# A polynomial-sketch attention fused with a SiLU feed-forward: one planned order for all engines, block-transposed layouts, one SiLU per two banks

## The chip, the cores and the metric

The kernel runs on one core of one Trainium2 chip. The metric is device time in microseconds (us) of one execution. "Profile" is a page and a trace of one execution, taken by the hardware profiler. Engines in it: PE is TensorE's matmuls, PEld its weight loads, DVE is VectorE, ACT is ScalarE, POOL is GpSimd, SP is SyncE (here it only issues DMAs). L352 is line 352 of the kernel profiled.

## The reference, cut to what matters

```python
batch, n_heads, seq, head_dim = 4, 4, 1088, 32      # r = 8
# attention without softmax: phi(x) = outer(S1 x, S2 x), 64 features per head
q_p, k_p = phi(q), phi(k)
kv  = einsum('bhsf,bhsd->bhfd', k_p, v);  z = k_p.sum(axis=2)
num = einsum('bhsf,bhfd->bhsd', q_p, kv)
den = einsum('bhsf,bhf->bhs',  q_p, z)[..., None] + 1e-06
x   = (num / den).transpose(0, 2, 1, 3).reshape(4352, 128)
# feed-forward
h = x @ w_in              # 128 -> 2048
g = h * sigmoid(h)        # SiLU
out = g @ w_out           # 2048 -> 128
```

The feed-forward has 2048 hidden columns, 16 tiles of 128 partitions, for 4352 tokens: 68 blocks of 128 x 1024. "Block" means such a block of `h` from here on; both kernels hold it in one PSUM tile of 2 x 512 fp32 columns (`h_ps`; `psA` or `psB`), and a half of such a tile is called a bank here.

## The kernel before

Attention runs batch by batch in tiles of 128 tokens, in fp32, with bf16 outer products shared by VectorE and GpSimd. The leftover 64 tokens of each batch (1088 = 8 x 128 + 64) are tiles of their own. Then comes the feed-forward, in chunks of 512 tokens; a scheduler may move its work up between the attention's. Its inner loop:

```python
for jp in range(NJ // 2):
    h_ps = psA.tile([P, 2, CH], FP32, name="h_ps", tag="h")          # two of these
    for jj in range(2):
        nc.tensor.matmul(h_ps[:, jj, :ntok], w_in_bf[:, j * P: (j + 1) * P], xT[:, t0: t0 + ntok], ...)
    s_sb = moe.tile([P, 2, CH], BF16, name="s_sb", tag="s")
    nc.scalar.activation(out=s_sb[:, :, :ntok], in_=h_ps[:, :, :ntok], func=ACT.Sigmoid)
    g_j = moeg.tile([P, 2, CH], BF16, name="g_sb", tag="g")
    nc.vector.tensor_tensor(out=g_j[:, :, :ntok], in0=h_ps[:, :, :ntok], in1=s_sb[:, :, :ntok], op=ALU.mult)
# ... 16 matmuls into outT_ps, a VectorE block transpose, 4 stores
```

and the projection of the queries, 128 tokens at a time, in fp32:

```python
nc.tensor.matmul(pq_ps[:nt, i, :], QT[:, t * P: t * P + nt], WQb, start=True, stop=True)   # 96 columns
```

## Time and profile before

Two runs: 198.16 and 195.95 us, median 197.06.

| what | value | where it is read |
|---|---|---|
| busiest engine | VectorE, 68% of the span | page, busy time |
| first sigmoid | 46.3 us | source view of its line |
| sigmoid, 128 x 1024 | 1.02 us | groups by line |
| multiply, 128 x 1024 | 1.21 us | groups by shape |
| DMA packets under 512 B | 71,424 of 72,075 | page, slices |

From the page of the kernel before: the span, each engine's busy time, and some rows of the span cut into 40 equal slices (4.9 us each). A digit is the busy share in tenths; PEclk is the granted TensorE clock in tenths of full speed.

```profile
span 196.7 us, 2161 instructions
...
PE 130.4 (66%) x674; PEld 73.1 (37%) x684; DVE 134.3 (68%) x239; ACT 95.5 (49%) x134; POOL 45.3 (23%) x100
...
PE   1085479744875999865767744859885757657660
...
DVE  4335644783678372998779897675478787787961
ACT  2001011347665233777755668363566757576560
PEclk9999999999998555999999999576999999999998
...
DMA packets 72075, 11.15 MB, mean 57 GB/s; under 512 B 71424, under 2 KB 71424, under 8 KB 71936
```

No engine is near full, so waiting sets the time. ScalarE does little in the first nine slices: the feed-forward has not begun. From slice 14 on the clock is at half for some slices, and again later.

From the page, the chain that ended last (by line) and the two costliest groups. Columns of a group: line, engine, operation, output<-input, shape, count | busy us, mean ns | idle us before it and what ended the idle time.

```profile
DVE g_sb L357 17%; ACT s_sb L355 12%; SPq L155 10%; SPq L147 10%; PE h_ps L352 8%; PE outT_ps L362 6%; SPq L164 5%; PE pq_ps L251 4%; PE pk_ps L184 3%; DVE o_tt L366 2%; DMA Qxx<-in_q_dram 2%; PE num_ps L305 1%; PE zacc L195 1%; DVE qp_b L290 1%; PE qpt_ps L299 1%
...
L357 DVE TENSOR_TENSOR g_sb<-h_ps,s_sb 128x1024 bf16<-128x1024 f32 (+1 forms) x72 | 81.3, 1154 | 19.8 <-ACT s_sb L355 18.9
L355 ACT ACTIVATE s_sb<-h_ps 128x1024 bf16<-128x1024 f32 (+1 forms) x72 | 70.1, 977 | 36.0 <-PE h_ps L352 31.0
```

The multiply is 81.3 of VectorE's 134.3 us. VectorE waits for the sigmoid (18.9 us in all), the sigmoid waits for `h` (31.0 us), and the matmul for `h` waits for the multiply (22.6 us by the page), which is the last to read the bank pair: a ring.

From the timeline of the kernel before, two pairs of 512-column matmuls (start us, duration us):

```profile
50.33 1.06 PE L352 MATMUL h_ps<-xT,w_in_bf 128*128 128x512 bf16 x2
...
143.74 0.59 PE L352 MATMUL h_ps<-xT,w_in_bf 128*128 128x512 bf16 x2
```

The same pair took 1.06 us and 0.59 us. A duration here is longer than the step from one matmul to the next: a single such matmul takes 0.38 us in the second state and 0.63 in the first (in the changed kernel's warm-up). So the step is about 1.06 - 0.63 = 0.43 us in the first case and 0.59 - 0.38 = 0.21 in the second. The first pair ran at half clock, although PEclk shows 9 at 50 us: the trace holds no clock record before about 52 us, and the row shows full speed until the first record. For the first part of a trace the matmuls' own spacing has to be read.

### The profile page before, as it was taken

What the parts mean: (1) busy time and instruction counts of PE and PEld (TensorE: products, weight loads), DVE (VectorE), ACT (ScalarE), POOL (GpSimd) and SP (SyncE); (2) the same over time, 40 slices, a digit from 0 to 9 for tenths busy, and PEclk for the clock granted to TensorE, in tenths of its full rate; (3) what the DMA queues carried; (4) which work ended last, traced back from release to release, by engine and by line L of the source; (5) the groups of instructions that cost most, each with busy time, mean ns of one, the idle gap of its engine ahead of it and who ended that gap; (6) DMA issues with size and microseconds to landing.
All of it is one profiled execution on the core that took longest, in us unless ns stands there. A gap on an engine that the chain in (4) does not pass through costs nothing.

```text
span 196.7 us, 2161 instructions
## 1 busy us (share of the span) xinstructions
PE 130.4 (66%) x674; PEld 73.1 (37%) x684; DVE 134.3 (68%) x239; ACT 95.5 (49%) x134; POOL 45.3 (23%) x100
## 2 busy tenths in 40 slices
PE   1085479744875999865767744859885757657660
PEld 1074468521322765422226522723331212212330
DVE  4335644783678372998779897675478787787961
ACT  2001011347665233777755668363566757576560
POOL 1173263871000431540007360170000000000000
PEclk9999999999998555999999999576999999999998
DMA  2989799779994000003000000003213012030031
GB/s 40 146 133 146 117 217 309 128 118 154 131 139 68 7 0 0 2 4 50 3 0 0 2 0 3 0 0 53 35 19 53 0 21 36 0 55 0 0 53 27
DMA packets 72075, 11.15 MB, mean 57 GB/s; under 512 B 71424, under 2 KB 71424, under 8 KB 71936
## 3 DMA queue, kind: packets, MB, share of 16 engines
q1 hardware_dynamic: 72064, 11.02, 38.1%
q8 instruction: 5, 0.08, 0.2%
q14 instruction: 6, 0.05, 0.1%
HBM read 8.79 MB, written 2.23 MB: 56 GB/s over the span
## 4 chain that ended last, share of the span: by engine, by line
SPq 26%; PE 25%; DVE 22%; ACT 15%; issue 5%; DMA 2%; POOL 2%; DVEq 0%; ACTq 0%; POOLq 0%
DVE g_sb L357 17%; ACT s_sb L355 12%; SPq L155 10%; SPq L147 10%; PE h_ps L352 8%; PE outT_ps L362 6%; SPq L164 5%; PE pq_ps L251 4%; PE pk_ps L184 3%; DVE o_tt L366 2%; DMA Qxx<-in_q_dram 2%; PE num_ps L305 1%; PE zacc L195 1%; DVE qp_b L290 1%; PE qpt_ps L299 1%
## 5 line engine op out<-in xcount | busy, mean ns | idle before, releaser
L357 DVE TENSOR_TENSOR g_sb<-h_ps,s_sb 128x1024 bf16<-128x1024 f32 (+1 forms) x72 | 81.3, 1154 | 19.8 <-ACT s_sb L355 18.9
L355 ACT ACTIVATE s_sb<-h_ps 128x1024 bf16<-128x1024 f32 (+1 forms) x72 | 70.1, 977 | 36.0 <-PE h_ps L352 31.0
L352 PE MATMUL h_ps<-xT,w_in_bf 128*128 128x512 bf16 (+1 forms) x138 | 42.9, 393 | 24.2 <-DVE g_sb L357 22.6
L362 PE MATMUL outT_ps<-g_sb,w_out_bf 128*128 128x512 bf16 (+1 forms) x140 | 43.7, 395 | 8.6 <-DVE g_sb L357 6.9
L352 PEld LDWEIGHTS <-w_in_bf 128*128 128x128 bf16 x144 | 14.2, 104 | 43.1 <-issue 26.4
L362 PEld LDWEIGHTS <-w_out_bf 128*128 128x128 bf16 x144 | 14.4, 103 | 25.9 <-issue 15.6
L201 POOL TENSOR_TENSOR kp_b<-pk_sb 128x256 bf16<-128x256 f32 x16 | 12.5, 802 | 43.8 <-ACT pk_sb L188 43.8
L184 PE MATMUL pk_ps<-WK,KT 128*128 128x64 f32 (+1 forms) x72 | 15.6, 381 | 8.4 <-DVE KT L175 8.4
L201 DVE TENSOR_TENSOR kp_b<-pk_sb 128x256 bf16<-128x256 f32 (+1 forms) x20 | 11.6, 614 | 11.0 <-ACT pk_sb L188 10.6
L251 PE MATMUL pq_ps<-WQb,QT 128*128 128x96 f32 (+1 forms) x72 | 16.8, 394 | 1.2 <-ACT pq_sb L258 1.2
L184 PEld LDWEIGHTS pk_ps<-WK,KT 128*128 128x128 f32 (+1 forms) x72 | 13.9, 283 | 10.0 <-DVE KT L175 9.5
L188 ACT ACTIVATE pk_sb<-pk_ps 128x256 f32<-128x256 f32 x8 | 3.1, 383 | 29.0 <-PE pk_ps L184 28.9
L220 POOL CAST vbf<-vraw 128x128 bf16<-128x128 f32 (+1 forms) x36 | 12.5, 366 | 14.9 <-DMA vraw<-in_v_dram 14.4
L251 PEld LDWEIGHTS pq_ps<-WQb,QT 128*128 128x128 f32 (+1 forms) x72 | 13.7, 281 | 4.0 <-ACT pq_sb L258 3.4
L290 DVE TENSOR_TENSOR qp_b<-aqs,pq_sb 128x256 bf16<-128x256 f32 (+1 forms) x20 | 10.8, 574 | 1.2 <-POOL aqs L282 0.6
L290 POOL TENSOR_TENSOR qp_b<-aqs,pq_sb 128x256 bf16<-128x256 f32 x16 | 11.3, 727 | 0.6
L258 ACT ACTIVATE pq_sb<-pq_ps 128x384 f32<-128x384 f32 x8 | 3.9, 490 | 14.6 <-PE pq_ps L251 11.7
L299 PE MATMUL qpt_ps<-ident_bf,qp_b 128*128 128x128 bf16 (+1 forms) x72 | 7.7, 244 | 5.0 <-ACT xT L308 4.7
L366 DVE STREAM_TRANSPOSE o_tt<-outT_ps 128x512 f32<-128x512 f32 (+1 forms) x9 | 6.1, 681 | 6.4 <-PE outT_ps L362 5.6
L299 PEld LDWEIGHTS <-qp_b 128*128 128x128 bf16 (+1 forms) x72 | 5.3, 108 | 9.9 <-issue 6.7
L308 ACT ACTIVATE xT<-num_ps 128x512 bf16<-128x512 f32 (+1 forms) x12 | 5.7, 475 | 6.1 <-PE num_ps L305 6.1
L195 PE MATMUL zacc<-pk_sb 128*32 128x32 f32 (+1 forms) x72 | 5.9, 233 | 4.0 <-ACT pk_sb L188 2.8
(69 smaller groups left out, 87.6 us busy)
## 6 DMA issues: line engine op xcount, KB each, us to landing
Kxx<-in_k_dram SPq DMA_DIRECT2D x16, 136.0 KB, 3.9
Qxx<-in_q_dram SPq DMA_DIRECT2D x16, 136.0 KB, 4.1
vraw<-in_v_dram SPq DMA_DIRECT2D x32, 64.0 KB, 3.2
out_dram<-o_tt SPq DMA_DIRECT2D x32, 64.0 KB, 2.0
w_in_f<-in_moe_w_in_dram SPq DMA_DIRECT2D x1, 1024.0 KB
vraw<-in_v_dram SPq DMA_DIRECT2D x4, 32.0 KB, 2.3
out_dram<-o_tt SPq DMA_DIRECT2D x4, 32.0 KB, 1.7
L_111<-in_S_dram SPq DMA_DIRECT2D x4, 1.0 KB
```

The source lines that it names most:

```text
L147: nc.sync.dma_start(Kxx[D * h: D * (h + 1), :, :], sap)
L155: nc.sync.dma_start(vt[:nt], v[b, :, t * P: t * P + nt, :].rearrange("h s d -> s h d"))
L184: nc.tensor.matmul(pk_ps[:nt, i, :], KT[:, t * P: t * P + nt], WK, start=True, stop=True)
L201: beng.tensor_tensor(out=kp[:nt], in0=_insert_bcast(ak4, 2, R), in1=_insert_bcast(bk4, 1, R), op=ALU.mult)
L220: nc.gpsimd.tensor_copy(out=vb[:nt], in_=Vraw[t][:nt])
L251: nc.tensor.matmul(pq_ps[:nt, i, :], QT[:, t * P: t * P + nt], WQb, start=True, stop=True)
L290: beng.tensor_tensor(out=qp[:nt], in0=_insert_bcast(aqs[:nt, i], 2, R), in1=_insert_bcast(bq4, 1, R), op=ALU.mult)
L299: nc.tensor.transpose(qpt_ps[:, p, c0: c0 + nt], in_, ident_bf[:nt, :nt])
L352: nc.tensor.matmul(h_ps[:, jj, :ntok], w_in_bf[:, j * P: (j + 1) * P], xT[:, t0: t0 + ntok], start=True, stop=True)
L355: nc.scalar.activation(out=s_sb[:, :, :ntok], in_=h_ps[:, :, :ntok], func=ACT.Sigmoid)
L357: nc.vector.tensor_tensor(out=g_j[:, :, :ntok], in0=h_ps[:, :, :ntok], in1=s_sb[:, :, :ntok], op=ALU.mult)
L362: nc.tensor.matmul(outT_ps[:, :ntok], w_out_bf[:, j, :], g_sb[j // 2][:, j % 2, :ntok], start=(j == 0), stop=(j == NJ - 1))
```

## The change

The intent: take the multiply and its PSUM read out of the ring, batch the attention's small operations, make every feed-forward block full, and fix one order of instructions for all engines.

The diff rewrites nearly the whole kernel; this is its core, with cuts marked `# ...`.

```diff
+class Plan:                       # a list scheduler: every op has an engine, an assumed cost and a due time
+    def order(self):
+        # ... for each op whose inputs are planned: earliest start t from engine, inputs, free banks
+                if best is None or (t < best[0] - 1e-9) or (t <= best[0] + 1e-9 and (o.due, o.idx) < best[3]):
+                    best = (t, o, got, (o.due, o.idx))
+        # ... the ops sorted by planned start are then emitted in that order on all engines
-            nc.scalar.activation(out=s_sb[:, :, :ntok], in_=h_ps[:, :, :ntok], func=ACT.Sigmoid)
-            nc.vector.tensor_tensor(out=g_j[:, :, :ntok], in0=h_ps[:, :, :ntok], in1=s_sb[:, :, :ntok], op=ALU.mult)
+                A_.activation(out=gt[int(s[0][1:])], in_=hp, func=ACTF.Silu)
+            a = op(f"S_{i}_{s_}", "ACT", 0.92, fa, [l1], due + 0.93 * s_ + 0.5, need=[("g", 1)], frees=[l1])
+            l2 = op(f"L2_{i}_{s_}", "PE", 0.435, f2, [a, wo[...], seq.get("l2")], due + 0.93 * s_ + 1.5, ...)
+    for i in range(9):             # warm-up matmuls on zeros
+        wk.append(op(f"warm{i}", "PE", 0.43, lambda s: mm(bank(7), warm[:, 0:128], warm), [warmz], -20 + i * 0.01))
+    def proj8(name, W, src, deps, due):          # batches 1 to 3: 8 tiles of 64 rows x 32 columns of the array
+        # ...
+                    mm(bank(s[P])[32 * j:32 * j + 32, 0:256].rearrange("p (g x) -> p g x", g=2),
+                       W[64 * P:64 * P + 64].rearrange("p x h i -> p (x h i)"),
+                       src[64 * P:64 * P + 64, :, j].rearrange("p g c t -> p g (c t)"),
+                       tile_position=(64 * P, 32 * j))
+            dt = op(f"QD{b}{hf}", "SP", 0.5, lambda s, i=i, hf=hf: nc.sync.dma_start_transpose(
+                out=QPT[i][:, 4 * hf:4 * hf + 4].rearrange("p c q t -> p (c q) t"),
+                in_=qp[i][:, 4 * hf:4 * hf + 4].rearrange("p c h f -> p (c h f)")), ...)
+    chunk("r", col, 256, xr, None, t0)           # the 4 x 64 leftover tokens as one last chunk
```

Four consecutive tokens lie beside each other on a partition now, so a load moves runs of 256 or 512 bytes. The weights and V are cast to bf16 by the DMA (from the POOL queue). VectorE transposes between token and feature layout, which the program lays out in blocks of 32. Batch 0 takes another way, with TensorE transposes and full-array projections, 128 tokens at a time; it has to be first and quick. "Head" is the time until the first SiLU.

## The prediction

> **What bounds the kernel now.** The page gives no engine above 68% of the 196.7 us span (VectorE 134.3 us, TensorE 130.4, ScalarE 95.5); waiting sets the time.
>
> (1) Head: by the source view, the first sigmoid starts at 46.3 us. Attention of batches 0 and 1 goes first, behind 128-byte DMA packets (71,424 of 72,075 under 512 B; the 40-slice row shows the DMA busy until about 60 us) that one queue issues.
>
> (2) Then 64 full and 8 half blocks. Between 140 and 186 us the timeline shows 1.3 to 1.45 us per 1024 columns: matmul, sigmoid (1.02 us), VectorE multiply out of the same PSUM pair (1.21 us), only then is the bank free. By group, the multiply costs 81.3 us and is 17% of the chain of waits; "h_ps waits for g_sb" is 20.9 us. Between 62 and 80 us only 4 sigmoids ran: fp32 attention matmuls (8 take 1.5 to 2 us) came first, at a granted clock of 0.53.
>
> **Removed.** The multiply and one PSUM read per block: SiLU is one ScalarE pass. POOL's products go (45.3 us POOL; VectorE's 128x256 products took 0.64 us beside POOL, 0.41 at least). Weight casts move into the DMA. 68 full blocks, no half ones. Input packets of 256 to 512 B.
> **Added.** 6 DMA transposes (no duration in this trace), head transposes on TensorE, block transposes on VectorE (128x512: 0.68 us), warm-up matmuls.
>
> **Costs after.** ScalarE: consecutive 128x1024 activations start about 0.92 us apart in the chain view: 68 x 0.92 = 63 us. [...] So SiLU should cost what sigmoid did. TensorE: four 512-column matmuls 0.213 us apart (timeline, full clock): 0.86 us a block, 58 us in all. Estimated extra per batch from trace pieces: KV products 18 x 83 ns = 1.5, z 0.7, projections 2, numerators 0.9, about 5.5 us; three batches, plus later parts of batch 0 and leftovers (7): 58 + 17 + 7 = 82 us. VectorE: about 14 us per batch of 18 to 19, not the limit. TensorE becomes the limit, ScalarE second.
>
> **Sum.** First SiLU at about 16 us (K by 5, then some fifteen short dependent operations); stream 84 us with few waits; tail 4 us (matmuls, copy, store about 2). Total **104 us**, 8-in-10 range **94 to 118**. Chances: faster by over 2% 0.98, within 2% 0.01, slower 0.01.
>
> **What would show it.** First SiLU at 13 to 20 us; 68 SiLUs of 1.0 to 1.03 us, mean start to start 1.15 to 1.3 us; TensorE over 80% busy in the stream, clock near 1 (it fell to 0.5 before after slices with little matmul work); VectorE 60 to 70%, POOL almost nothing; ScalarE waits for h (TensorE), not VectorE; the chain mostly matmuls of the two layers.
>
> **What would make it wrong.** DMA transposes landing after 4 us or more: [...] The order follows assumed costs; one underestimated item blocks an engine while others have work. The 64x32 tiles may not overlap (projections 3 us, not 1: +10 us). Casting loads from POOL could be slow: head over 20 us. Half clock after a stall (0.9 us more per block). On the good side, less TensorE work than I add up: 92 us.

The sum came to 16 + 84 + 4 = 104 us. The 63 us for ScalarE come from the 0.92 us of the trace. No trace of the kernel before has a SiLU, so that it should cost what sigmoid did was my assumption. The 4 us, the 3 us for projections and the 20 us for casting loads are fears, not measurements; what came of them is told under "Why the prediction was wrong". The fall of the clock to 0.5 is in the trace: TensorE was busy for 0.70 of the 2 us from 60 to 62 us, and from about 62 to 79 us the clock was at half.

## The result, and the profile after

Two runs: 121.17 and 121.28 us; median 121.22. The ratio to the kernel before is 0.6152 (95% interval 0.6003 to 0.63). All ratios here are the mean time of one kernel's fast runs over that of the other's fast runs of the same rounds, so not quite the ratio of the medians. Faster was right, by a wide margin; 121.2 us lies outside the range of 94 to 118.

From the page of the changed kernel, the same parts as before, with slices of 3.0 us:

```profile
span 119.4 us, 2011 instructions
...
PE 106.1 (89%) x745; PEld 59.6 (50%) x753; DVE 60.0 (50%) x149; ACT 71.6 (60%) x80; POOL 17.3 (14%) x33
...
PE   5978999997997899999999999989998998898930
...
ACT  0442210100568965609877777888979989889840
PEclk9995555555599999999999999999999999999998
...
DMA packets 43177, 10.58 MB, mean 89 GB/s; under 512 B 34688, under 2 KB 43168, under 8 KB 43168
...
PE ps L256 28%; DMA KL<-in_k_dram 20%; ACT gt L496 17%; PE psA L256 9%; PE psB L256 7%; DMA Qr<-in_q_dram 4%; DMA QPT<-qp 3%; DMA K<-in_k_dram 3%; DVE KT L683 1%; SPq L261 1%; DVE AQ L717 1%; DVE kp L367 1%; DVE Mq L729 0%; ACT orest L527 0%; ACTq L496 0%
```

TensorE is now the full engine, as predicted. But the PEclk row has eight slices at half clock, about 9 to 33 us, and ScalarE's row starts in earnest only at the eleventh slice. (The chain's DMA share lies before 33 us, where it is followed back along the loading queue. TensorE was busy all along, and the first experiment moves the head without touching a load.)

The source view of the SiLU line. Columns: operation, count, duration ns min/median/max, first and last start us, shapes:

```profile
L496 ACT ACTIVATE gt<-psB x34: 1017/1021/1030, 31.3 to 112.2; 128x1024 bf16<-128x1024 f32 x34
L496 ACT ACTIVATE gt<-psA x34: 1017/1024/1030, 32.2 to 113.5; 128x1024 bf16<-128x1024 f32 x34
```

So 68 SiLUs of 1.02 us as predicted, but the first starts at 31.3 us, not 16. The last ends at 113.5 + 1.02 = 114.5: the stream took 83.2 us, against 84 predicted. The tail took 119.4 - 114.5 = 4.9 us, against 4. Against the prediction: head +15.3, stream -0.8, tail +0.9, and 1.8 us between the span and the device time, in all 17.2. The miss is the head.

Three windows in the head. Columns: window, its length, busy us (instructions) of PE, PEld, DVE, ACT and POOL, granted clock, DMA share, GB/s:

```profile
10.00:15.00 5.00, 4.54 (x33) 3.89 (x33) 3.30 (x7) 1.45 (x4) 2.84 (x5) 0.50 1.36 207
15.00:20.00 5.00, 5.00 (x24) 4.82 (x24) 2.51 (x6) 0.37 (x1) 3.30 (x5) 0.50 1.43 226
20.00:25.00 5.00, 5.00 (x51) 3.80 (x51) 3.47 (x10) 0.59 (x1) 2.12 (x3) 0.50 1.55 210
```

TensorE is busy for nearly the whole of each window, at half clock. I had taken it that a busy TensorE keeps its full clock; this one did not. The timeline of the same stretch shows with what it is busy (start us, duration us):

```profile
14.35 1.97 PE L256 MATMUL psA<-Wh,Q0T 128*128 128x64 f32 x8
...
16.81 1.97 PE L256 MATMUL ps<-Wh,Q0T 128*128 128x64 f32 x8
18.57 1.86 PE L256 MATMUL psA<-MQ,Q0T 128*128 128x32 f32 x8
...
25.31 0.63 PE L256 MATMUL ps<-V,kp 128*128 128x64 bf16 x8
```

These are mostly fp32 matmuls of 64 and 32 columns, each behind an fp32 weight load (the eight of the first line took 1.78 us): the PEld column above is 4.82 of 5 us from 15 to 20 us. The KV matmuls of batch 0, which the first chunk needs, come only at 25.3 us, behind the projections of later queries. The trace shows no wait for V there: the two loads of batch 0's V had landed by 12.8 us (issued at 4.6 and 5.4, landed 7.3 to 7.5 us later). It was the planned order that put them late.

Late in the stream, where no attention is left, the timeline of the changed kernel shows this order:

```profile
96.81 1.02 ACT L496 ACTIVATE gt<-psB 128x1024 bf16<-128x1024 f32 x1
96.96 0.59 PE L256 MATMUL ps<-gt,w_out 128*128 128x512 bf16 x2 [0.26 <-ACT gt L496]
...
97.39 0.59 PE L256 MATMUL psA<-xT,w_in 128*128 128x512 bf16 x2
...
98.08 1.02 ACT L496 ACTIVATE gt<-psA 128x1024 bf16<-128x1024 f32 x1 [0.26 <-PE psA L256]
...
99.00 1.02 ACT L496 ACTIVATE gt<-psB 128x1024 bf16<-128x1024 f32 x1
```

After the SiLU of psA ends (96.91), TensorE first does the second-layer matmuls of that block and only then refills psA; ScalarE idles 0.26 us in each pair. A pair of blocks takes 99.00 - 96.81 = 2.19 us, 1.10 per block, though SiLUs on end start 0.92 us apart (98.08 and 99.00).

### The profile page after: what moved, and what is told of

It is laid out like the page before. It is cut to its first block, busy times and chain, and to the rows that moved or that the text cites. A ratio compares the mean times of both kernels' runs of the same rounds, so it can differ in the third digit from the quotient of the medians.

```text
span 119.4 us, 2011 instructions
## 1 busy us (share of the span) xinstructions
PE 106.1 (89%) x745; PEld 59.6 (50%) x753; DVE 60.0 (50%) x149; ACT 71.6 (60%) x80; POOL 17.3 (14%) x33
## 2 busy tenths in 40 slices
DMA packets 43177, 10.58 MB, mean 89 GB/s; under 512 B 34688, under 2 KB 43168, under 8 KB 43168
## 4 chain that ended last, share of the span: by engine, by line
PE 44%; DMA 29%; ACT 17%; DVE 3%; issue 2%; SPq 1%; ACTq 0%; another core or an unknown queue 0%
PE ps L256 28%; DMA KL<-in_k_dram 20%; ACT gt L496 17%; PE psA L256 9%; PE psB L256 7%; DMA Qr<-in_q_dram 4%; DMA QPT<-qp 3%; DMA K<-in_k_dram 3%; DVE KT L683 1%; SPq L261 1%; DVE AQ L717 1%; DVE kp L367 1%; DVE Mq L729 0%; ACT orest L527 0%; ACTq L496 0%
## 5 line engine op out<-in xcount | busy, mean ns | idle before, releaser
L496 ACT ACTIVATE gt<-psB 128x1024 bf16<-128x1024 f32 x34 | 34.7, 1021 | 18.2 <-PE psB L256 17.7
L496 ACT ACTIVATE gt<-psA 128x1024 bf16<-128x1024 f32 x34 | 34.8, 1022 | 8.6 <-PE psA L256 6.1
L256 PE MATMUL ps<-gt,w_out 128*128 128x512 bf16 (+1 forms) x141 | 36.3, 355 | 3.2 <-ACT gt L496 2.8
L256 PEld LDWEIGHTS <-w_in 128*128 128x128 bf16 x160 | 15.5, 100 | 16.1 <-issue 3.3
L256 PEld LDWEIGHTS <-w_out 128*128 128x128 bf16 x144 | 12.8, 97 | 18.2 <-issue 10.6
L256 PE MATMUL psB<-xT,w_in 128*128 128x512 bf16 (+1 forms) x81 | 20.6, 351 | 0.6 <-ACT gt L496 0.4
L256 PE MATMUL psA<-xT,w_in 128*128 128x512 bf16 (+1 forms) x74 | 19.8, 358 | 0.2
L367 DVE TENSOR_TENSOR kp<-AB 128x512 bf16<-128x512 f32 x16 | 10.4, 680 | 3.4 <-ACT AB L450 3.4
L367 DVE TENSOR_TENSOR qp<-aqs,AQ 128x512 bf16<-128x512 f32 (+1 forms) x14 | 9.5, 719 | 0.1
L261 POOL DMA_DIRECT2D V<-in_v_dram x8 | 6.1, 759 | 2.7 <-DMA w_out<-in_moe_w_out_dram 2.7
```

The costliest lines, as they stand in the source:

```text
L256: P_.matmul(out_, lhsT, rhs, start=start, stop=stop, **kw)
L261: return op(name, eng, 1.0 if eng == "POOL" else 0.5, lambda s: e.dma_start(dst, src), deps, due, xfer=kb * 1.024 / rate)
L367: V_.tensor_tensor(out=dst, in0=bcast(a, 2, R), in1=bcast(b_, 1, R), op=ALU.mult)
L496: A_.activation(out=gt[int(s[0][1:])], in_=hp, func=ACTF.Silu)
```

## The experiments

Every run gave correct results. The kernels in one group ran on the same chip with their own runs of the kernel before. That kernel ran in two ways itself: on two of the four chips its fast runs took 192.4 to 194.8 us (clock 0.93 to 0.97), on the other two 197.5 to 199.6 (0.90 to 0.925). So ratios of different groups differ by some 2 to 3% for this reason alone, and the record calls the six verdicts from the first two chips "unclear". Between groups I compare the times of fast runs, and leave small differences open.

Theory 1: the half clock holds the head back, because the work there does not keep the clock up: it was 0.50 from 10 to 25 us, with TensorE busy for 4.5 to 5.0 us of each 5 (the reason I named was fp32 matmuls and transposes; few columns per weight load was my next guess; no run showed either). Theory 2 (rival): the head waits for the V load and for the planned order, and the clock is a side effect.

### Keep TensorE streaming in the head

The order is unchanged. One bf16 matmul on zeros goes in front of every TensorE group before the first chunk, into the bank that the group then overwrites.

```diff
+        head = True
         for o in plan.order():
+            if o.name == "L1_0_0":
+                head = False
+            if head and o.eng == "PE" and o.slots:
+                for _ in range(1):
+                    mm(bank(o.slots[0])[:, 0:256], warm[:, 0:128], warm[:, 0:256])
             o.fn(o.slots)
```

> One 128x256 bf16 matmul on constant data goes before every TensorE group of the head (about 32 of them), into the bank that the group then overwrites; order unchanged. Theory 1 (half clock holds the head back, because fp32 matmuls and transposes do not keep the clock up): granted clock 1.0 from about 7 us on, first SiLU at 22 to 26 us instead of 31.3, time 113 to 117 us instead of 121. Theory 2 (the head waits for the V load and for the planned order, not for the clock): first SiLU at 30 to 33 us whatever the clock, time 120 to 124.

Four runs: 116.01, 115.73, 115.11 and 116.89 us; the last was slow. Ratio 0.5817. The granted clock on its page:

```profile
PEclk9999999999999999999999999999999999999995
```

As the row shows full speed before the first record too, the spacing has to confirm it. From its timeline, two of the pieces shown above:

```profile
13.34 1.00 PE L256 MATMUL psA<-Wh,Q0T 128*128 128x64 f32 x8
...
20.17 0.40 PE L256 MATMUL ps<-V,kp 128*128 128x64 bf16 x8
```

They took 1.97 and 0.63 us before. And the source view of its SiLUs on psB, where the first one runs:

```profile
L496 ACT ACTIVATE gt<-psB x34: 1017/1022/1030, 25.6 to 107.1; 128x1024 bf16<-128x1024 f32 x34
```

The first SiLU came at 25.6 us instead of 31.3. Work was added, no load and no order was changed, and the kernel became 5.5 us faster (medians of the fast runs: 121.2 to 115.7). That the half clock held the head back is shown, for 5.7 us of it. These are net: the 25 added matmuls took about 0.11 us each (they stand 0.11 us before the next matmul in this trace), some 2.7 us by my estimate.

The same with 512 columns (`0:256` becomes `0:512`):

> As the 256-column run, with 512 columns: more activity, but 7 us more work. Theory 1: clock 1.0 in the head, first SiLU at 23 to 27 us, time 114 to 118. If the 256-column ones were too few to hold the clock, this one does. Theory 2: first SiLU at 32 us or later, time 122 to 126.

Runs 116.72, 117.91, 118.22, 117.90 us; ratio 0.5921. Clock 0.994, first SiLU at 26.8 us: in this group 256 columns were enough, and 512 only cost time (115.7 to 117.9 us, fast medians). In later orders 256 were not always enough.

### V first

V of batch 0 is issued before anything else on the POOL queue, and the four small S2 loads go to the SP queue.

```diff
-    V0 = [dma("POOL", f"V0{g}", ..., 192, -9.5 + 0.01 * g) for g in range(2)]
-    L2s = [dma("POOL", f"L2{h}", ..., 4, -9.6)
+    V0 = [dma("POOL", f"V0{g}", ..., 192, -11 + 0.01 * g) for g in range(2)]
+    L2s = [dma("SP", f"L2{h}", ..., 4, -8.5)
-    Vrl = [rest_load("POOL", v, Vr, 0, -9.4, "Vr")]
+    Vrl = [rest_load("POOL", v, Vr, 0, -10.9, "Vr")]
```

> V of batch 0 is issued first on the POOL queue, the four small S2 loads move to the SP queue; the plan then puts the KV matmuls of batch 0 some 5 us earlier. Theory 2: first SiLU at 24 to 27 us, time 115 to 118. Theory 1: TensorE is busy all the time at half clock, so the first SiLU comes only as much earlier as work has moved behind it: 28 to 30 us, time 119 to 121.

Runs 125.36, 125.35, 125.35 us, and 127.58 slow; ratio 0.6307. From the source view of its SiLUs:

```profile
L496 ACT ACTIVATE gt<-psB x35: 1017/1024/1025, 29.1 to 118.0; 128x1024 bf16<-128x1024 f32 x35
```

The first SiLU came at 29.1 us, within the 28 to 30 of theory 1; theory 2's 24 to 27 is refuted. The total rose by 4 us, which neither theory had. The scheduler had built another order for the rest too. From ScalarE's timeline:

```profile
49.22 1.02 ACT L496 ACTIVATE gt<-psB 128x1024 bf16<-128x1024 f32 x1 [0.70 <-PE psB L256]
59.03 1.02 ACT L496 ACTIVATE gt<-psB 128x1024 bf16<-128x1024 f32 x1 [8.79 <-remote]
```

ScalarE idled for 8.8 us in one piece, while TensorE and VectorE worked off attention of later batches. Changing one load's due time reordered the middle of the kernel. That the idle piece is what cost the 4 us was not tested.

### First layer before second layer

Raising the due time of the second-layer matmuls lets the scheduler refill a bank pair first.

```diff
-            l2 = op(f"L2_{i}_{s_}", ..., due + 0.93 * s_ + 1.5, ...)
+            l2 = op(f"L2_{i}_{s_}", ..., due + 0.93 * s_ + 2.4, ...)
```

> The due time of the second-layer matmuls is raised by 0.9 us, so first-layer matmuls for block s+2 go in front of the second-layer matmuls of block s. Theory: in the last 25 us, where nothing else runs, the pair of blocks takes 2.19 us because SiLU and TensorE take turns; with the new order SiLU runs back to back at 0.92 to 0.95 us per block, 1.85 per pair; some 22 blocks gain 0.15 us each: time 117 to 119 us, head unchanged (first SiLU at 31 us). Rival (PSUM or a fixed wait sets the 1.10 us): no change.

Runs 112.97 us (fast, clock 0.966), 114.97 (slow, 0.928), 120.31 and 120.66 (slow, 0.875). The times go with the clock: only the fast run's mean clock is far above the changed kernel's 0.895. The order's own worth can't be read from that, so the two edits were put together:

> Both the 256-column matmuls in the head and the first layer in front of the second. If the two gains are independent: first SiLU at 25.6 us, pairs of blocks in the last 25 us in 1.85 to 1.95 us instead of 2.19, time 111 to 113 us, and no slow runs from clock dips as long as the clock stays at 1.0. If the clock dips again in the stream because the waits are shifted: 114 to 117.

Runs 113.63 and 112.38 us fast, 114.41 and 114.56 slow; ratio 0.5799. By the fast medians it gains 2.7 us (115.7 to 113.0), by the ratios next to nothing (0.5817 and 0.5799, intervals overlapping: 0.578 to 0.5854 and 0.5706 to 0.5893), and the two ran on different chips. So a gain in time is not shown. (The one fast run of the order alone points to one: 112.97 us, on the chip where the filler alone took 115.1 to 116.0.) The first SiLU came at 26.8 us, not 25.6, and the clock fell to half from 24.2 to 27.6 us, so the expectation of a steady clock failed too. (The profiled run is a slow one, of 114.41 us; its mean clock, 0.985, is that of the fast run of 113.63.) The mechanism shows in its timeline of ScalarE late in the stream:

```profile
94.98 1.04 ACT L496 ACTIVATE gt<-psB 128x1024 bf16<-128x1024 f32 x1
...
95.88 1.05 ACT L496 ACTIVATE gt<-psA 128x1024 bf16<-128x1024 f32 x1
...
96.79 1.07 ACT L496 ACTIVATE gt<-psB 128x1024 bf16<-128x1024 f32 x1
...
97.69 1.08 ACT L496 ACTIVATE gt<-psA 128x1024 bf16<-128x1024 f32 x1
```

SiLUs start 0.90 us apart with no idle time, instead of 1.10. But part of it was lost elsewhere: at 85.5 us ScalarE idled 2.7 us in one piece. TensorE was then at the numerators of the next tokens, for which the last chunks need x, and waited 0.19 and 0.44 us for their DMA transposes. The attention of the last batch had come too late in this order.

### How long is the chain of the head itself?

With the clock held up, V first, and the later queries of batch 0 and the keys of batch 1 put behind the first chunk:

```diff
-            d, rc = q0_sketch(name, 1, [Q0b], t0 - 5, "x", "DVE")
+            d, rc = q0_sketch(name, 1, [Q0b, xA], t0 - 5, "x", "DVE")
-                KLl[b] + hist.get(("kt", i), []), kd))
+                KLl[b] + [xA] + hist.get(("kt", i), []), kd))
```

(and both edits above, V first and 256 columns.)

> With the clock held up in the head, V of batch 0 is fetched first, and the second half of batch 0's queries and all of batch 1's keys wait for the first chunk. Theory: of the 15 us by which the first SiLU was later than predicted, about 5.7 are the clock, and most of the rest is V landing late and other work put in front: first SiLU at 18 to 21 us. Rival: the chain of short operations itself takes that long: 24 to 26 us. The total may well not fall (113 to 120), since what is put off comes back in the stream, where TensorE is the limit.

```profile
L496 ACT ACTIVATE gt<-psA x35: 1017/1024/1026, 22.7 to 113.0; 128x1024 bf16<-128x1024 f32 x35
```

First SiLU at 22.7 us, between the theory's 18 to 21 and the rival's 24 to 26. Runs 120.40, 120.11, 120.05 us, 125.59 slow; ratio 0.6168. So of the 15.3 us, 5.7 are the clock, 2.9 (25.6 - 22.7) V first and the work put off (tried apart only in part: V first alone brought 2.2 us at half clock, 31.3 to 29.1), and the remaining 6.7 belong to the chain as it ran here: it is longer than I had added up. And the total did not gain: the stream behind it took 114 - 22.7, about 91 us. From 22 to 45 us, where the work that was put off ran, TensorE was busy for 22.6 us of 23. But the order of the stream had changed as well (from 45 to 70 us ScalarE was busy for 14.4 us, against 17.9 with the filler alone), so that TensorE's work by itself kept the total up is argued, not shown.

### How much is SiLU, how much the rest?

The changed kernel with the sigmoid and the multiply put back:

```diff
-                A_.activation(out=gt[int(s[0][1:])], in_=hp, func=ACTF.Silu)
+                A_.activation(out=sgt[int(s[0][2:])], in_=hp, func=ACTF.Sigmoid)
+                V_.tensor_tensor(out=gt[int(s[0][1:])], in0=hp, in1=sgt[int(sg.slots[0][2:])], op=ALU.mult)
# ... (two buffers for the sigmoid, and the multiply as an op of its own on VectorE)
```

> The changed kernel with the sigmoid and the VectorE multiply of the kernel before in place of SiLU. VectorE then has 60 + 68 x 1.21 = 142 us of work: it becomes the limit, time 155 to 170 us; SiLU is then 35 to 50 of the 76 us gained.

163.84 and 162.25 us; ratio 0.8368. In the trace of 162.1 us ScalarE waited 62.9 us (44.1 and 18.8) for matmuls into psB and psA, which the multiply now frees. VectorE's own work was about 142 us by the estimate above: the 60.0 us of the changed kernel and 68 multiplies of 1.21, as in the kernel before.

And the kernel before with SiLU alone:

```diff
-            nc.scalar.activation(out=s_sb[:, :, :ntok], in_=h_ps[:, :, :ntok], func=ACT.Sigmoid)
-            nc.vector.tensor_tensor(out=g_j[:, :, :ntok], in0=h_ps[:, :, :ntok], in1=s_sb[:, :, :ntok], op=ALU.mult)
+            nc.scalar.activation(out=g_j[:, :, :ntok], in_=h_ps[:, :, :ntok], func=ACT.Silu)
```

> The kernel before with SiLU in place of sigmoid and multiply, nothing else. The last stretch (140 to 190 us), where the multiply sets the pace, should fall from 1.35 to about 1.1 us per block; the first SiLU stays at 46 us, and the stretches at half clock stay: time 165 to 185 us. If SiLU alone were the whole gain it would come near 121.

172.23 and 169.82 us; ratio 0.8777. The first SiLU stayed at 46.1 us. Each half alone takes 12% and 16% off the time; together they take 38%. With the new layouts alone VectorE is the limit by that estimate; with SiLU alone the head and the attention at half clock stay. Neither can pay in full without the other.

### What keeps the clock up?

fp32 matmuls of 64 columns in place of the bf16 ones:

```diff
+    warmf = T([128, 128], FP32, "warmf")
-                    mm(bank(o.slots[0])[:, 0:256], warm[:, 0:128], warm[:, 0:256])
+                    mm(bank(o.slots[0])[:, 0:64], warmf, warmf[:, 0:64])
# ... (and warmf is set to zero)
```

> In the place of the 256-column bf16 matmuls in the head, fp32 ones of 64 columns with fp32 weights: [...] fp32 with a long weight load. If any streaming counts as activity: clock 1.0 in the head and 116 to 119 us. If fp32 work counts little, as the head itself suggests (TensorE over 95% busy from 10 to 30 us at half clock): clock stays at 0.5 from about 10 us, first SiLU at 33 to 37 us, time 123 to 128.

118.73 and 118.70 us. The clock on the page:

```profile
PEclk9999999995999999999999999999999999999996
```

(The "long weight load": in the trace of the kernel before, 128x128 weights took 292 and 294 ns in fp32 and 103 and 104 in bf16, means over both clocks. And TensorE was busy for 18.7 of the 20 us from 10 to 30 us of the changed kernel, 93%, not over 95.) The clock held until 26 us and fell for one slice or so (26.4 to 29.8 us); first SiLU at 29.2. So fp32 as such is not what lets the clock fall. I had thought it likely that fp32 counts little; that is refuted. Nor is it few columns per weight load, since this filler has as few as the head's own matmuls.

bf16 with 64 columns:

> bf16 matmuls of 64 columns instead of 256 in the head. If the presence of bf16 work is enough: clock 1.0, first SiLU at 25 us, 115 us. If the share of time that columns stream through the array decides: too few, clock 0.5, first SiLU at 31 to 33 us, 121 to 123 us.

One run of 115.43 us (clock 0.973), one of 123.04 (slow, clock 0.892), whose page is this:

```profile
PEclk9996555555599999999999999999999999999996
```

So with 64 columns the same program had a mean clock of 0.973 once and half clock in the head once. No run varies the columns alone, so that they decide is not shown. What in the work of the head lets the clock fall is open.

Without the nine warm-up matmuls:

```diff
         for o in plan.order():
+            if o.eng == "PE" and o.name.startswith("warm"):
+                continue
             o.fn(o.slots)
```

> The nine warm-up matmuls are left out, the plan is the same. In the trace they raise the clock only for 6.3 to 9.7 us, and they hold the first transposes up from about 4.0 to 5.1 us. Theory: without them the head runs wholly at half clock but starts a little earlier: first SiLU at 31 to 33 us, 121 to 123 us, that is within 1 to 2 us of the changed kernel, so they bring next to nothing. Rival (they are what keeps the head going): 125 or more.

Runs 120.60, 120.53 fast, 122.48, 122.73 slow; the fast ones are no slower than the changed kernel's 121.17 and 121.28. In the changed kernel the clock was at full from about 6 us, after the warm-up, and at half again from about 9 (the windows of its trace say 9.1, not 9.7). The warm-up bought nothing. The kept trace of this run (120.60 us) holds two lessons:

```profile
PEclk9999998555589999999999999999999999999999
...
8.23 3.67 PE L256 MATMUL psB<-Wh,K0T 128*128 128x64 f32 x16 [0.77 <-ACT KrT L431]
...
17.58 1.10 PE L256 MATMUL ps<-Wh,Q0T 128*128 128x64 f32 x8
```

At 8.2 us the row says full speed, but 16 matmuls took 3.67 us, where the run with 256 columns took 1.00 for 8: the clock was at half, and the first record came only at 16.6 us. (That may be why the two slow runs have 0.999 and 0.996 in their records; they left no trace.) And from 16.6 to 20 us the clock was at full, 1.10 us for the eight matmuls that took 1.97 in the changed kernel, with the same narrow fp32 work and no filler at all. So this narrow work ran at both clocks. In the clock records of the traces of both kernels, every stretch between two changes lasts a whole multiple of 3.41 us (in the changed kernel 3.41 at full, then 23.9 at half, then 85.3 at full). Why one program runs both ways was not tested.

### A version that beats both

First layer first, V first, 256 columns in the head, and the due times of the attention moved until the planner's own estimate was lowest. The planner ranks orders; it gives no time of the chip.

```diff
-  ... due + 0.93 * s_ + 1.5, ...        -  kd = t0 - 13        -  qd_ = t0 - 9.5
+  ... due + 0.93 * s_ + 3.3, ...        +  kd = t0 - 18        +  qd_ = t0 - 14
```

> All that helped, with the due times of the plan moved until its own estimate was lowest: first layer first, V of batch 0 first, 256-column matmuls in the head, attention of the next batch 5 us earlier in the plan. If V first gains another 3 us on the head and TensorE stays full: first SiLU at 21 to 24 us, time 108 to 112. If TensorE's sum of work is the limit and the head only moves work into the stream: 112 to 115, as with the first two changes alone.

109.74 and 110.37 us fast (clock 0.996 and 0.994); 114.74 and 114.91 slow (0.949, 0.950), with half clock from 9 to 19 us. Ratio 0.5704. Two groups of times, about 4.8 us apart. If the clock makes them, more columns in the head should leave one group:

> The best order so far, with 512-column matmuls in the head in place of 256-column ones. In its fast runs the best order took 110 us with the clock near 1.0 (mean 0.995), in its others 114.8 with the clock at half from about 10 to 20 us. If only the clock makes that difference and 512 columns hold it in every run: all four runs within 109 to 112.5 us, clock 0.98 or more. If something else makes the two states: still two groups 4 us apart.

> Two 256-column matmuls in front of each group: as many columns as one of 512, so the same clock and 109 to 113 us. If one long matmul counts for more than two shorter ones, the clock drops in some runs here, not with 512.

512 columns: 111.62, 112.01, 112.08, 111.66 us, ratio 0.5651. Two of 256: 112.09, 111.85, 110.97, 111.01, ratio 0.5629. One group each, no run with a mean clock below 0.992. The clock on the page with 512 columns:

```profile
PEclk9999999999999999999999999999999999999999
```

(in its timeline the eight Wh,Q0T matmuls take 1.00 us, so the head did run at full clock) and the source view of its SiLUs:

```profile
L496 ACT ACTIVATE gt<-psB x33: 1018/1023/1086, 25.9 to 103.1; 128x1024 bf16<-128x1024 f32 x33
L496 ACT ACTIVATE gt<-psA x35: 1018/1023/1084, 26.8 to 104.0; 128x1024 bf16<-128x1024 f32 x35
```

The head is no shorter than with the first edit alone (25.9 and 25.6 us), yet the stream behind it took 79 us (25.9 to 104.0 + 1.1) instead of 84 (25.6 to 108.4 + 1.0). Some 10 us better than the changed kernel, of which about half is the clock, if the 5.5 us of the first experiment carry over to this order.

## Why the prediction was wrong

**The step that failed** is "First SiLU at about 16 us (K by 5, then some fifteen short dependent operations)". It measured 31.3 us.

- *Clock, 5.7 us.* I predicted "clock near 1" and named half clock only "after a stall". The head has no such stall: TensorE is over 90% busy from 10 to 25 us and still at half clock. The kernel before had shown it: between 62 and 80 us TensorE was busy for 17.4 of 18 us, with fp32 attention matmuls above all, at a mean clock of 0.53. I took it for the result of little work ahead of it (0.70 us busy from 60 to 62); but the clock stayed at half for 17.1 us of this work. That the half clock delayed the head is what the filler matmuls show: 31.3 to 25.6 us, and that after paying for themselves. Why the clock stays down in this work is open.
- *The order, with V first, 2.9 us.* The order put later queries in front of the KV matmuls (the run with work put off). V itself was not late: it had landed by 12.8 us, and the KV matmuls ran at 25.3. I had feared slow casting loads; they were not what the head waited for. (With some 210 GB/s moving, the casting loads of V, 128 KB each from the POOL queue, landed 7.3 to 12.7 us after issue; loads of K of the same size without a cast, from the SP queue, took 6.2 to 10.0. So the cast is not shown to be the reason.)
- *The chain itself, 6.7 us.* "K by 5" was right (its two loads landed at 3.8 and 4.7 us). I gave the fifteen steps 16 - 5 = 11 us; the run with work put off had 22.7 - 5 = 17.7 us for them. Its trace shows where they went: K's transposes run from 5.3, behind the warm-up matmuls, to 7.8 us; the sketches of K and of the first queries from 9.4 to 14.1; KV and the sum z to 16.9; denominators, quotient and the last transposes from 17.7 to 21.5; the first layer, at half clock again, to 22.7. 17 filler matmuls are in it (about 1.8 us by my estimate, at 0.11 each). Each step costs an operation and a hand-over (TensorE's waits in that timeline are 0.23 to 1.34 us each), and several come in twos. This part is a difference of measured numbers, not an experiment of its own.

**A second fault lies under it.** I added head, stream and tail as if they were separate. TensorE is nearly full over the whole program (89%): shortening the head by putting work off (22.7 us) left the total at 120. The more useful sum, I think, is TensorE's work over the whole program, each stretch at its own clock.

**What held:**

- *TensorE becomes the limit, ScalarE second*: 89% and 60% busy, and VectorE down to 50%. VectorE in the stream was 52% busy (windows from 31 to 114 us), below my 60 to 70%.
- *SiLU costs what sigmoid did*: 1021 to 1024 ns in the median against 1023, and 0.90 to 0.92 us from start to start where nothing waits.
- *Stream 84 us*: 83.2. It is right in part by luck: TensorE's work in it was less than my 82 us (windows from 31 to 114 us add up to 78 us busy), and the turn-taking of the two layers, which I did not see in the diff, filled the rest. Mean SiLU spacing 83.2/68 = 1.22 us, in the predicted 1.15 to 1.3.
- *The feared DMA transposes* did little harm: one of 128 x 1024 bf16 elements took 1.27 us to issue and landed after 3.3 us; TensorE's weight loads waited 0.5 us for them in all, and they are 3% of the chain.
- *The feared 64x32 tiles* cost less than feared: the eight of a batch's K projection took 0.66 us in all at full clock (for instance at 58.7 us), less than my 1 us.

## What to carry to other kernels

A TensorE that is busy all the time can be at half clock (here 5.00 us of 5 at 0.50, from 15 to 20 us): check the clock row and the matmul spacing. Where a stretch of narrow fp32 matmuls sits at half clock, try a few wide matmuls (zeros will do) between their groups: here one of 256 columns per group gave mean clocks of 0.976 to 0.998 and 5.5 us, but in another order 0.949 and 0.950 in two of four runs. So make several runs of each width: one program can run both ways. When one engine is nearly full over the whole program, add up its work over the whole span at the clock of each stretch; moving work out of the head did not shorten this one. In a queue that runs in the order it was given, as TensorE's did here (psA was free at 96.91 us, and its refill came at 97.39, behind the second layer), with two buffers, try refilling the freed buffer before consuming the result: here it closed ScalarE's gaps of 0.26 us, though a gain in the total by itself is not shown.
